# One contiguous run a partition for weights and output gates, and raw weight loads issued from ScalarE in an mLSTM + feed-forward kernel

## The chip, the cores and the metric

One core of one Trainium2 chip. The metric is the device time of the program in microseconds (us), the median over several executions. In the profile, PE is TensorE's matmuls and PEld its weight loads, DVE is VectorE, ACT ScalarE, POOL GpSimd, SP SyncE, which only issues transfers here. A name with a q behind it (SPq, ACTq) is that engine's instruction queue. Three engines issue transfers: SP, ScalarE and GpSimd.

## The reference, cut to what matters

```python
# mLSTM: batch 4, heads 8, 768 steps, head size 40
m_new = max(f + m, i);  f_stab = exp(f + m - m_new);  i_stab = exp(i - m_new)
C = f_stab * C + i_stab * outer(v, k);   n = f_stab * n + i_stab * k
y = sigmoid(o_gate) * (C q) / max(|n q|, 1)
# then on the 3072 x 320 result:
h = x @ w_in            # 320 x 2048
g = softplus(h)
out = g @ w_out         # 2048 x 320, float32 result
```

`w_in` and `w_out` arrive as float64; everything else is float32.

## The kernel before, in words

The 3072 tokens are cut into 24 steps of 128 (one batch and one chunk each; `ORDER` is their order), and three steps make a tile of 384 tokens. For each of the 8 tiles the feed-forward part runs over 16 blocks of 128 hidden columns: 8 matmuls of the block (L974, `hp`), softplus twice on ScalarE (L848, L849, `gh` and the full value), the remainder `gl` on VectorE (L852), and, two blocks later, 9 output matmuls (L942, `po`). A value is split into a high and a low part so that the fast matmul format keeps float32 accuracy.

The order of all work is written out by hand: TensorE's products of the blocks are counted (`tick(n)`), and every other piece of work is a generator that is resumed when the count reaches its place. `in_order` then fixes the order of the instructions on each engine as they were traced. So each engine, and SP's queue too, works strictly in this order: an instruction that waits holds what is behind it on its engine.

The mLSTM steps supply tile after tile. The first six (tiles 0 and 1) are plain steps, the others wide ones. For each step SP issues the decays `fb` (L421), two buffers of 128 partitions from a DRAM copy of the gates, which VectorE scans into the decay matrices `pw` (L430), further the queries and keys `qst`, `kst` (L369 and L370 in plain steps; in wide ones four copies of the high parts, L376, and two of the low parts, L390, from SBUF to SBUF) and the values `vt` (L405). The scores `sp` (L504) are multiplied into `pw` (L506). The wide steps' `iq` (L557), `y` (L560, L573) and `yq` (L568) give the step's output. `X` is the finished input of the feed-forward part: L619 (ScalarE) and L621 in plain steps, L605 and L607 in wide ones. `eg` holds the output gates of a tile, loaded from `oT` (L339) and put through a sigmoid (L345).

The weights are 16 tensors, 8 slices of `w_in` and 8 of `w_out`, each 128 partitions of 640 float64 values, loaded in the order of `tensors` into the raw buffers `wr` (three of them, `WB`, which the parts `lo` of tiles 3, 5 and 7 use later too). A slice of `w_in` takes three transfers (L221 once, L224 twice), a slice of `w_out` one (L227). A conversion (`single`, then `weights` or `weights_out`) makes float32 of the two 32-bit words of each value: ScalarE scales the high word into `mag` (L198) and the low word into `sg` (L201), VectorE puts in the sign from the high word (L203) and the shifted magnitude (L205). Then ScalarE casts the high part (L236, L240 or L251) and GpSimd forms the low part (L243, L245 or L253). The conversions run beside the blocks from 18 to about 129 us.

The first three loads are issued by `first_tile`, and its last line issues the fourth. After that a generator `fetch` stands beside each conversion and issues the next load, from SP, 8 counts behind the conversion's fourth piece of work, so behind L205, by which time the raw buffer has been read by ScalarE and VectorE.

A few transfers are issued by ScalarE already: `halves` (L1001, L1009) and most results `out` (L1022).

Of the kernel before, what the change touches and what calls it, by code (L numbers as in the profile page):

```python
# [8 lines left out]
F32 = mybir.dt.float32  # L9
F32R = mybir.dt.float32r  # L10
U32 = mybir.dt.uint32
AF = mybir.ActivationFunctionType
ALU = mybir.AluOpType
PSUM = bass.MemoryType.PSUM

B, H, S, D = 4, 8, 768, 40
L = 128
NG = 3
T = NG * L
NT = B * S // T  # L20
NC = S // L
HG = H // 2
DM = H * D
DFF = 2048
NF = DFF // 128
# [14 lines left out]
def mlstm_moe_kernel(  # L40
# [3 lines left out]
    vko: bass.AP,  # L44
    gates: bass.AP,
    oT: bass.AP,
    w_in: bass.AP,
    w_out: bass.AP,
    out: bass.AP,
):  # L50
    nc = tc.nc
    words = []
    if w_in.dtype != F32:
        words = [2]
        w_in = w_in.bitcast(U32).rearrange("r (f w) -> r f w", w=2)
        w_out = w_out.bitcast(U32).rearrange("r (e w) -> r e w", w=2)
    wdt = w_in.dtype

    cpool = ctx.enter_context(tc.tile_pool(name="cpool", bufs=1))
    p1 = ctx.enter_context(tc.tile_pool(name="p1", bufs=1))  # L60
# [129 lines left out]
    def single(src, n):  # L190

        if not words:
            return src
        lo_w, hi_w = src[:, :, :, 0], src[:, :, :, 1]
        shape = list(hi_w.shape)
        mag = stage.tile(shape, F32, tag="mag", bufs=MB, name=f"mag{n}")

        nc.scalar.activation(mag, hi_w.bitcast(F32), AF.Copy, scale=2.0**-112)  # L198
        yield
        sg = stage.tile(shape, U32, tag="sg", bufs=3, name=f"sg{n}")  # L200
        nc.scalar.activation(sg, lo_w, AF.Copy, scale=2.0**-29, bias=-0.4375)  # L201
        yield
        nc.vector.scalar_tensor_tensor(sg, hi_w, 0x80000000, sg, op0=ALU.bitwise_and, op1=ALU.bitwise_or)  # L203
        yield
        nc.vector.scalar_tensor_tensor(sg, mag.bitcast(U32), 3, sg, op0=ALU.logical_shift_left, op1=ALU.bitwise_or)  # L205
        yield
        return sg.bitcast(F32)

    def rows(a):
        return a.rearrange("(c p) f w -> p c f w" if words else "(c p) f -> p c f", p=128)  # L210

    WB, MB = 3, 2
    raw = {}

    def load_weights(u, i):
        if (u, i) in raw:
            return
        if i == 0:
            cs = slice(u * 256, (u + 1) * 256)
            r = stage.tile([128, 5, 128] + words, wdt, tag="wr", bufs=WB, name=f"wr{u}")  # L220
            nc.sync.dma_start(r[:, 0:4].rearrange("p (c j) f w -> p c (j f) w", c=2), rows(w_in[0:256, cs]))  # L221
            for j in range(2):
                f = 2 * u + j
                nc.sync.dma_start(r[j * 64 : (j + 1) * 64, 4], w_in[256:320, f * 128 : (f + 1) * 128])  # L224
        else:
            r = stage.tile([128, 2, DM] + words, wdt, tag="wr", bufs=WB, name=f"wo{u}")
            nc.sync.dma_start(r, rows(w_out[u * 256 : (u + 1) * 256]))  # L227
        raw[u, i] = r

    def weights(u):  # L230

        cs = slice(u * 256, (u + 1) * 256)
        w = yield from single(raw[u, 0], f"i{u}")
        w2 = w[:, 0:4].rearrange("p (c j) f -> p c (j f)", c=2)
        los = []
        nc.scalar.copy(wih[:, 0:2, cs], w2)  # L236
        for i in range(2):
            c1 = slice((2 * u + i) * 128, (2 * u + i + 1) * 128)
            hi, lo = slice(i * 64, (i + 1) * 64), slice((1 - i) * 64, (2 - i) * 64)
            nc.scalar.copy(wih[hi, 2, c1], w[hi, 4])  # L240
            los.append((wih[lo, 2, c1], w[hi, 4], wih[hi, 2, c1]))
        yield
        nc.gpsimd.tensor_tensor(wil[:, :, cs], w2, wih[:, 0:2, cs], op=ALU.subtract)  # L243
        for d, x, y in los:
            nc.gpsimd.tensor_tensor(d, x, y, op=ALU.subtract)  # L245
        yield

    def weights_out(u):
        w = yield from single(raw[u, 1], f"o{u}")
        js = slice(2 * u, 2 * u + 2)  # L250
        nc.scalar.copy(woh[:, js, :], w)  # L251
        yield
        nc.gpsimd.tensor_tensor(wol[:, js, :], w, woh[:, js, :], op=ALU.subtract)  # L253
        yield

    Cst = {}
# [78 lines left out]
    def wide_gates(t):  # L335

        yield 0
        eg[t] = p2.tile([128, NG, 3, L], F32, tag="eg", name=f"eg{t}")
        nc.sync.dma_start(  # L339
            eg[t].rearrange("p g c t -> p (g c) t"),  # L340
            oT[t * NG : (t + 1) * NG].rearrange("g (c p) t -> p (g c) t", p=128),
        )
        yield GL
        nc.scalar.preload_act_table_set("sigmoid_and_others")
        nc.scalar.activation(eg[t], eg[t], AF.Sigmoid)  # L345
        nc.scalar.preload_act_table_set("softplus")
        yield GL
# [3 lines left out]
    eg = {}  # L351
# [287 lines left out]
    def first_tile():  # L639
        zs = z0, z1, z2 = [Step(s) for s in range(NG)]  # L640
        run = lambda g: [None for _ in g]

        def part(g):
            for r in g:
                if not r:
                    return

        keep_warm(7)
        p0, lg = first_gates(), later_gates()
        next(p0)  # L650
        next(lg)
        load(z0)
        load(z1)
        next(p0)
        next(lg)
        nc.sync.dma_start(fz_d[0], fg0[:NCHAIN])
        og = p2.tile([128, NH, DM], F32, tag="X", bufs=XB, name="og")

        def output_gates(i0, i1):
            for i in range(i0, i1):  # L660
                b, c = ORDER[i]
                nc.sync.dma_start(og[:, i], vko[b, c * L : (c + 1) * L, H * E + DM :])
            yield
            nc.scalar.activation(og[:, i0:i1], og[:, i0:i1], AF.Sigmoid)
            yield

        o0, o1 = output_gates(0, NG), output_gates(NG, NH)
        next(o0)
        load(z2)
        load_weights(0, 0)  # L670
        next(o1)
        load_weights(1, 0)
        load_weights(0, 1)
        for z in zs:
            z.sig = og[:, z.g].rearrange("p (h d) -> p h d", d=D)
        v0, v1, v2 = (values(z) for z in zs)
        s0, s1, s2 = ([scores(z, i) for i in range(2)] for z in zs)
        x0, x1, x2 = (split_x(z) for z in zs)

        def mms(g):  # L680
            while next(g, None) == 1:
                pass

        def seq(*gs):
            for g in gs:
                next(g, None)

        decays(z0)
        run(p0)
        mms(s0[0])  # L690
        mms(s0[1])
        decays(z1)
        mms(s1[0])
        mms(s1[1])
        load(steps[NG])
        decays(steps[NG])
        gate_values(z0)
        next(lg)
        next(lg)
        nc.scalar.preload_act_table_set("sigmoid_and_others")  # L700
        put_off(lg, GR[2])
        gate_values(z1)
        decay(z0)
        last_decays(z0)
        seq(*s0)
        next(v0)
        decay(z1)
        last_decays(z1)
        decays(z2)
        seq(o0, wparts)  # L710
        next(v0)
        seq(*s1)
        next(v1)
        mms(s2[0])
        mms(s2[1])
        gate_values(z2)
        decay(z2)
        last_decays(z2)
        next(v0)
        next(x0)  # L720
        next(v1)
        seq(o1)
        nc.scalar.preload_act_table_set("softplus")
        seq(*s2)
        next(v2)
        next(x0)
        next(v1)
        next(x1)
        keep_warm(8)
        seq(x0)  # L730
        next(wparts)
        next(x1)
        next(v2)
        seq(x1)
        next(wparts)
        next(v2)
        next(x2)
        keep_warm(4)
        next(wparts)
        seq(wparts)  # L740
        next(x2)
        seq(x2)
        for _ in wparts:
            pass
        for z in zs:
            state_values(z)
        for i in range(NG, NH):
            nc.sync.dma_start(sgp[i], og[:, i])
        fetch_next()
        return zs  # L750

    def plain_step(z):
# [105 lines left out]
    def convert(u, i):  # L858
        g = (weights_out if i else weights)(u)
        for w in (CO if i else CW):  # L860
            yield w
            next(g, None)

    def fetch(i):
        yield (CO if i else CW)[3] + 8
        fetch_next()

    def fetch_next():
        if len(raw) < NF:
            load_weights(*tensors[len(raw)])  # L870
# [17 lines left out]
    def start(g, base):  # L888
        nonlocal order
        order += 1  # L890
        resume(g, base, 0, order)
# [142 lines left out]
    with in_order():  # L1034
        for k, (u, i) in enumerate(tensors[AHEAD:]):
            if k < 2:
                at = (-8, -2)[k]
            else:
                at = (17 - 2 * 34, 26 - 34 + 10 * (u == 4))[i] + 34 * u if u < SPLIT // 2 else (160, 180)[i] + 38 * (u - SPLIT // 2)
            start(convert(u, i), at)  # L1040
            start(fetch(i), at)
        start(first_states(), 0)
        LEAD, TS = 174, 16 * 17
        EARLIER = 26
# [55 lines left out]
```

## Time and profile before

| | |
|---|---|
| median of 3 runs | 495.0 us (493.74 to 495.5) |
| the profiled execution | 498.18 us, its span 496.4 us |
| TensorE matmuls busy | 473.1 us, 95% of the span |
| VectorE, ScalarE, GpSimd busy | 325.1, 216.6, 222.7 us |
| transfers from SP's queue (q1) | 67.82 MB, 44738 packets |
| transfers from ScalarE's queue (q10) | 4.43 MB, 3888 packets |

Rows of a timeline read: start, duration, engine, line, operation, tile written <- tiles read, shape, count; in brackets the idle time of that engine before it and what ended it. Rows of waits read: engine and line that waited <- what ended the wait: us in total, how often, the longest. A row of stretches gives the stretch, its length, the busy time of each engine with its instructions, the granted TensorE clock as a share of full speed (PEclk), the mean busy share of the 16 DMA engines, and what they moved. Rows of a tile give the line, engine, operation and count, then shortest/median/longest in ns, and the first and last start in us. Releasers are inferred: where an instruction waits for several things, the one named is the one that came last by the profile.

### The profile page before, as it was taken

To read this page: it belongs to the slowest core of one execution; us is meant where nothing else is said; L and a number is where in the kernel's file an instruction comes from. 1 tells how busy PE (TensorE), PEld (TensorE's weight loads), DVE (VectorE), ACT (ScalarE), POOL (GpSimd) and SP (SyncE) were. 2 spreads that over 40 slices of the span, in tenths; PEclk is the share of its full clock that TensorE was granted. 3 is DMA by queue.
4 is the path that set the end of the run, shared out by engine and by line. 5 is a ranking of instruction groups with operands and counts; after the bars stand their busy time and mean duration, and the time that the engine had idled before them with its cause. 6 is when DMAs were issued, how large, how long until landed. Compare 5 with 4: busy or idle time off the path is not lost.

```text
span 496.4 us, 9346 instructions
## 1 busy us (share of the span) xinstructions
PE 473.1 (95%) x3444; PEld 451.9 (91%) x3444; DVE 325.1 (65%) x517; ACT 216.6 (44%) x424; POOL 222.7 (45%) x303
## 2 busy tenths in 40 slices
PE   8997899895999999999999999999999999999997
PEld 8986798894998889999999999999999999999996
DVE  7877785689377676695587577578568567542211
ACT  1665544596224632536343534254343632333332
POOL 7375667387656324743355352643384244010000
PEclk9998898899799999999999999999999999999999
DMA  6946895769735877558856684569755572001001
GB/s 191 279 136 171 235 292 168 209 197 207 208 107 138 243 205 205 163 182 209 221 153 180 189 223 149 167 190 213 217 159 174 142 204 89 17 23 41 0 1 40
DMA packets 52991, 81.10 MB, mean 163 GB/s; under 512 B 7906, under 2 KB 31634, under 8 KB 52946
## 3 DMA queue, kind: packets, MB, share of 16 engines
q1 hardware_dynamic: 44738, 67.82, 48.7%
q0 software_dynamic: 4320, 8.26, 6.4%
q10 hardware_dynamic: 3888, 4.43, 2.7%
q8 instruction: 27, 0.44, 0.4%
q14 instruction: 18, 0.15, 0.1%
HBM read 52.38 MB, written 8.80 MB: 123 GB/s over the span
## 4 chain that ended last, share of the span: by engine, by line
PE 75%; DVE 10%; DMA 8%; ACT 3%; issue 2%; SPq 2%; ACTq 0%; DVEq 0%
PE hp L974 33%; PE po L942 31%; PE yq L568 3%; PE sp L504 3%; DVE pw L430 3%; DMA fb<-fz_d 3%; PE cp L481 2%; PE iq L557 2%; DMA lok<-in_qk 2%; DMA wr<-in_w_in 1%; DMA y<-fc_d 1%; DMA vt<-in_vko 1%; PE yp L538 1%; DVE sgo L203 1%; DVE gl L852 1%
## 5 line engine op out<-in xcount | busy, mean ns | idle before, releaser
L974 PE MATMUL hp<-X,wih 128*128 128x384 f32 x768 | 185.1, 345 | 3.0 <-ACT X L619 1.8
L974 PEld LDWEIGHTS hp<-X,wih 128*128 128x128 f32 x768 | 134.4, 191 | 6.1 <-ACT X L619 2.3
L848 ACT ACTIVATE gh<-hp 128x384 fp32r<-128x384 f32 x128 | 62.7, 490 | 175.0 <-PE hp L974 156.3
L852 DVE TENSOR_TENSOR gl<-hp,gh 128x384 fp32r<-128x384 f32 x128 | 70.2, 549 | 60.0 <-ACT hp L849 59.7
L942 PE MATMUL po<-woh,gl 128*128 128x320 f32 x384 | 84.2, 314 | 0.1
L942 PE MATMUL po<-woh,gh 128*128 128x320 f32 x384 | 84.1, 316 | 0.2
L942 PE MATMUL po<-wol,gh 128*128 128x320 f32 x384 | 83.1, 316 | 0.0
L430 DVE TENSOR_TENSOR_SCAN pw<-fb,ident 128x512 f32<-128x512 f32 x48 | 72.5, 1551 | 2.5 <-DMA fb<-fz_d 1.9
L974 PE MATMUL hp<-X,wil 128*128 128x384 f32 x256 | 70.0, 347 | 0.0
L942 PEld LDWEIGHTS po<-woh,gh 128*128 128x128 f32 x384 | 66.0, 190 | 1.6 <-ACT gh L848 0.4
L942 PEld LDWEIGHTS po<-woh,gl 128*128 128x128 f32 x384 | 63.5, 191 | 0.6 <-DVE gl L852 0.4
L942 PEld LDWEIGHTS po<-wol,gh 128*128 128x128 f32 x384 | 62.9, 191 | 1.0 <-issue 0.9
L849 ACT ACTIVATE hp<-hp 128x384 f32<-128x384 f32 x128 | 62.3, 487 | 0.0
L580 POOL DMA_DIRECT2D yd<-y x36 | 20.8, 579 | 89.5 <-DVE y L573 87.7
L974 PEld LDWEIGHTS hp<-X,wil 128*128 128x128 f32 x256 | 46.8, 191 | 1.1 <-issue 1.0
L560 DVE TENSOR_TENSOR y<-iq,y 41x512 f32<-41x512 f32 x36 | 24.5, 682 | 29.9 <-PE iq L557 28.7
L504 PEld LDWEIGHTS sp<-qst,kst 120*128 120x128 f32 (+1 forms) x240 | 33.8, 199 | 9.1 <-DVE sgo L203 5.1
L504 PE MATMUL sp<-qst,kst 120*128 120x128 f32 (+1 forms) x240 | 34.3, 278 | 8.0 <-DMA lok<-in_qk 4.8
L605 ACT CAST X<-eg 128x384 fp32r<-128x384 f32 x18 | 9.2, 513 | 59.2 <-DVE eg L603 59.2
L506 DVE TENSOR_TENSOR pw<-sp,pw 128x512 f32<-128x512 f32 x48 | 31.9, 680 | 4.1 <-PE sp L504 3.8
L486 DVE TENSOR_TENSOR cn<-cn,cp 40x328 f32<-40x328 f32 x16 | 7.8, 486 | 33.9 <-POOL cn L472 31.3
L457 POOL TENSOR_TENSOR vw<-vt,gw 128x328 f32<-128x328 f32 x19 | 16.7, 883 | 27.6 <-DVE gw L451 27.3
(131 smaller groups left out, 602.2 us busy)
## 6 DMA issues: line engine op xcount, KB each, us to landing
fb<-fz_d SPq DMA_DIRECT2D x42, 256.0 KB
vt<-in_vko SPq DMA_DIRECT2D x23, 324.0 KB
qst<-hiq SPq DMA_DIRECT2D x36, 160.0 KB
kst<-hik SPq DMA_DIRECT2D x36, 160.0 KB
wo<-in_w_out SPq DMA_DIRECT2D x8, 640.0 KB
wr<-in_w_in SPq DMA_DIRECT2D x8, 512.0 KB
eg<-in_oT SPq DMA_DIRECT2D x6, 576.0 KB
yd<-y POOLq DMA_DIRECT2D x36, 96.0 KB, 3.5
```

Of the source, the lines that this page charges most:

```text
L430: nc.vector.tensor_tensor_scan(pw.rearrange(flat), fb.rearrange(flat), ident4.rearrange(flat), 0.0, ALU.mult, ALU.add)
L457: nc.gpsimd.tensor_tensor(z.vw, v1, z.gw.broadcast_to([128, H, E]), op=ALU.mult)
L504: nc.tensor.matmul(sp[:, j, :], z.kst[:, h, :], z.qst[:, h, :], start=True, stop=True)
L506: nc.vector.tensor_tensor(z.pws[i], sp, z.pws[i], op=ALU.mult)
L560: nc.vector.tensor_tensor(y, iq, y, op=ALU.mult)
L568: nc.tensor.matmul(yq[e0:e1, p, :], z.via[:, h * E : h * E + e1 - e0], z.pws[h // HG][:, h % HG, :], start=True, stop=True)
L580: nc.gpsimd.dma_start(rows[i], z.y[i * PP : i * PP + EP])
L848: nc.scalar.activation(gh, hp, AF.Softplus)
L849: nc.scalar.activation(hp, hp, AF.Softplus)
L852: nc.vector.tensor_tensor(gl, hp, gh, op=ALU.subtract)
L942: nc.tensor.matmul(po[j], a[:, j * 128 : (j + 1) * 128], w[:, f, :], start=(first and left[j] == 2), stop=(last and left[j] == 0),)
L974: nc.tensor.matmul(hp, a, r, start=(i == 0), stop=(i == len(seq) - 1))
```

## The change

The weights lie in DRAM as one array `wts`, tensor by tensor, each with one contiguous run of 5,120 bytes a partition; so a load is one transfer for both kinds. `oT` is laid out the same way, one run of 4,608 bytes a partition for a tile. The loads from the fourth on are issued by ScalarE (`nc.scalar`) inside `single`, directly behind L201, the last read of the raw buffer by ScalarE. VectorE's sign operation takes the sign from `mag`, the scaled high word, so that VectorE no longer reads the raw buffer. The generators `fetch` and the fetch at the end of `first_tile` go. (The branches for `not words` are for float32 weights and do nothing here.)

```diff
         sg = stage.tile(shape, U32, tag="sg", bufs=3, name=f"sg{n}")
         nc.scalar.activation(sg, lo_w, AF.Copy, scale=2.0**-29, bias=-0.4375)
-        yield
-        nc.vector.scalar_tensor_tensor(sg, hi_w, 0x80000000, sg, op0=ALU.bitwise_and, op1=ALU.bitwise_or)
+        fetch_next()
+        yield
+        nc.vector.scalar_tensor_tensor(sg, mag.bitcast(U32), 0x80000000, sg, op0=ALU.bitwise_and, op1=ALU.bitwise_or)
         yield
...
-        if i == 0:
-            cs = slice(u * 256, (u + 1) * 256)
-            r = stage.tile([128, 5, 128] + words, wdt, tag="wr", bufs=WB, name=f"wr{u}")
-            nc.sync.dma_start(r[:, 0:4].rearrange("p (c j) f w -> p c (j f) w", c=2), rows(w_in[0:256, cs]))
-            for j in range(2):
-                f = 2 * u + j
-                nc.sync.dma_start(r[j * 64 : (j + 1) * 64, 4], w_in[256:320, f * 128 : (f + 1) * 128])
-        else:
-            r = stage.tile([128, 2, DM] + words, wdt, tag="wr", bufs=WB, name=f"wo{u}")
-            nc.sync.dma_start(r, rows(w_out[u * 256 : (u + 1) * 256]))
+        r = stage.tile([128, (2, 5)[i == 0], (DM, 128)[i == 0]] + words, wdt, tag="wr", bufs=WB, name=f"w{i}{u}")
+        (nc.scalar if len(raw) >= WB and words else nc.sync).dma_start(r.rearrange("p c f w -> p (c f w)" if words else "p c f -> p (c f)"), wts[2 * u + i])
         raw[u, i] = r
...
         nc.sync.dma_start(
-            eg[t].rearrange("p g c t -> p (g c) t"),
-            oT[t * NG : (t + 1) * NG].rearrange("g (c p) t -> p (g c) t", p=128),
+            eg[t].rearrange("p g c t -> p (g c t)"),
+            oT[t],
         )
...
             nc.sync.dma_start(sgp[i], og[:, i])
-        fetch_next()
         return zs
...
-    def fetch(i):
-        yield (CO if i else CW)[3] + 8
-        fetch_next()
-
     def fetch_next():
         if len(raw) < NF:
             load_weights(*tensors[len(raw)])
...
             start(convert(u, i), at)
-            start(fetch(i), at)
```

On the host the two weight arrays are transposed and stacked into `wts`, and `oT` is transposed.

More of the change, by code (lines that the diff above doesn't have):

```diff
@@ L46, in mlstm_moe_kernel @@
     oT: bass.AP,
-    w_in: bass.AP,
-    w_out: bass.AP,
+    wts: bass.AP,
     out: bass.AP,
@@ L52, in mlstm_moe_kernel @@
     words = []
-    if w_in.dtype != F32:
+    if wts.dtype != F32:
         words = [2]
-        w_in = w_in.bitcast(U32).rearrange("r (f w) -> r f w", w=2)
-        w_out = w_out.bitcast(U32).rearrange("r (e w) -> r e w", w=2)
-    wdt = w_in.dtype
+        wts = wts.bitcast(U32)
+    wdt = wts.dtype
     cpool = ctx.enter_context(tc.tile_pool(name="cpool", bufs=1))
@@ L207, in single @@
         return sg.bitcast(F32)
-    def rows(a):
-        return a.rearrange("(c p) f w -> p c f w" if words else "(c p) f -> p c f", p=128)
     WB, MB = 3, 2
@@ L245, in weights @@
             nc.gpsimd.tensor_tensor(d, x, y, op=ALU.subtract)
+        if not words:
+            fetch_next()
         yield
@@ L253, in weights_out @@
         nc.gpsimd.tensor_tensor(wol[:, js, :], w, woh[:, js, :], op=ALU.subtract)
+        if not words:
+            fetch_next()
         yield
@@ L1083 @@
         "gates": gates,
-        "oT": np.concatenate([oT, oT[:, DM - 64 :]], axis=1),
-        "w_in": inputs["moe_w_in"].reshape(H, D, DFF).transpose(1, 0, 2).reshape(DM, DFF),
-        "w_out": inputs["moe_w_out"],
-    }
+        "oT": np.concatenate([oT, oT[:, DM - 64 :]], axis=1).reshape(NT, NG, 3, 128, L).transpose(0, 3, 1, 2, 4).reshape(NT, 128, -1),
+    }
+    w = inputs["moe_w_in"].reshape(H, D, DFF).transpose(1, 0, 2).reshape(DM, NF // 2, 2, 128)
+    last = w[256:].transpose(2, 0, 1, 3).reshape(128, NF // 2, 1, 128)
+    w_in = np.concatenate([w[0:128], w[128:256], last], axis=2).transpose(1, 0, 2, 3)
+    w_out = inputs["moe_w_out"].reshape(NF // 2, 2, 128, DM).transpose(0, 2, 1, 3)
+    arrays["wts"] = np.stack([a.reshape(NF // 2, 128, -1) for a in (w_in, w_out)], axis=1).reshape(NF, 128, -1)
     arrays = {f"in_{n}": np.ascontiguousarray(a) for n, a in arrays.items()}
```

## The prediction

> **What bounds the kernel now.** I read the page first, then the table of stretches, then what TensorE waits for before and after 130 us, and last the timelines of the two stretches in which it waits for a transfer.
>
> ```profile
> span 496.4 us, 9346 instructions
> PE 473.1 (95%) x3444; PEld 451.9 (91%) x3444; DVE 325.1 (65%) x517; ACT 216.6 (44%) x424; POOL 222.7 (45%) x303
> ```
> ```profile
> core 0: us, PE busy (x) PEld busy (x) DVE busy (x) ACT busy (x) POOL busy (x), PEclk, DMA share, GB/s
> 30.00:40.00 10.00, 8.19 (x79) 7.09 (x77) 8.93 (x9) 6.25 (x12) 8.91 (x12) 1.00 0.14 42
> 60.00:70.00 10.00, 9.86 (x75) 9.06 (x75) 8.81 (x14) 5.25 (x10) 8.99 (x7) 0.88 1.02 261
> 100.00:110.00 10.00, 9.87 (x74) 9.09 (x74) 9.24 (x12) 9.92 (x15) 8.40 (x10) 1.00 0.64 203
> 120.00:130.00 10.00, 5.40 (x20) 5.43 (x21) 6.76 (x9) 3.85 (x8) 9.17 (x10) 0.69 0.87 212
> 200.00:300.00 100.00, 100.00 (x760) 96.20 (x759) 70.29 (x113) 44.13 (x86) 49.04 (x75) 1.00 0.70 192
> ```
> ```profile
> PE sp L504 <- DMA lok<-in_qk: 4.8, 1, 4.8
> PE pg L177 <- DVE d L168: 2.7, 1, 2.7
> PE sp L504 <- DVE pw L506: 2.2, 1, 2.2
> PE hp L974 <- ACT X L619: 1.8, 2, 1.5
> PE yq L568 <- DVE y L560: 1.5, 1, 1.5
> ```
>
> TensorE is the bound: busy for all of 200 to 300 us. It can only be made faster where it stands still, and that is where the weights are still being loaded and converted, up to about 130 us. The third fence (TensorE's waits from 20 to 130 us) sums to 13.0 us. After each long wait the granted clock is down too: 0.88 in 60 to 70 us, 0.69 in 120 to 130 us. What the change saves on VectorE, SP or the DMA engines counts only if it shortens one of those rows; what it adds on ScalarE counts only if it lengthens one.
>
> **Edits that I cost at nothing.**
>
> ```profile
> L224 SPq DMA_DIRECT2D wr<-in_w_in x16: 465/558/882, 11.5 to 96.4; - x16
> L203 DVE SCALAR_TENSOR_TENSOR sgo<-wo,sgo x8: 812/831/1352, 33.7 to 123.0; 128x640 uint32<-128x640 uint32 x8
> L205 DVE SCALAR_TENSOR_TENSOR sgo<-mago,sgo x8: 804/960/1605, 41.0 to 123.9; 128x640 uint32<-128x640 uint32 x8
> L339 SPq DMA_DIRECT2D eg<-in_oT x6: 478/486/1097, 91.4 to 374.6; - x6
> L345 ACT ACTIVATE eg<-eg x6: 1166/1167/1169, 107.0 to 387.1; 128x1152 f32<-128x1152 f32 x6
> ```
>
> The sign operation now reads the scaled word, as L205 does, in place of every second word. The minima are 812 and 804 ns, so the stride costs nothing to remove; with L205's median it would be 0.13 us dearer, 2 us over 16 and mostly beside TensorE's work. I take 0. The gates as one run: the first issue is at 91.4 us and the first reader at 107.0, so 15 us cover it; at most the issue time falls, and it could not lose more than those 15 us. The 16 second and third issues of the first weight matrix go (0.56 us each, 9 us of SP's time). For the three loads that stay on SP none of the waits above ends in a load, so 0. What these 9 us are worth later belongs to the stalls.
>
> **The stall at 58 us.**
>
> ```profile
> 39.38 0.35 SPq L166 DMA_DIRECT2D fz_d<-fg  x1
> 39.82 0.39 SPq L227 DMA_DIRECT2D wo<-in_w_out  x1
> 44.14 0.42 SPq L221 DMA_DIRECT2D wr<-in_w_in  x1
> 44.61 1.14 SPq L224 DMA_DIRECT2D wr<-in_w_in  x2
> 47.18 0.90 SPq L421 DMA_DIRECT2D fb<-fz_d  x2
> ```
> ```profile
> 31.68 0.79 ACT L201 ACTIVATE sgo<-wo 128x640 uint32<-128x640 uint32 x1
> ```
> ```profile
> 53.40 2.80 DVE L430 TENSOR_TENSOR_SCAN pw<-fb,ident 128x512 f32<-128x512 f32 x2 [1.87 <-DMA fb<-fz_d]
> ```
>
> Each conversion still issues the load three ahead of it; only the place in the conversion and the queue change. SP works in order. The decay broadcast fb is issued behind two weight loads, which themselves stand behind a store that waits for VectorE. The scan waits 1.87 us for fb, and the 2.2 us wait of the scores is the end of that chain (scan, product L506, scores). With the change the load of 44.14 is issued by ScalarE when its activation at 31.68 is done, at 32.5 us, and that of 39.82 one conversion before; both fall where the DMA share is 0.14. So fb is issued 0.42 + 1.14 = 1.6 us sooner and two loads of 655 KB (128 partitions of 5,120 B), 3.1 us each at the 212 GB/s of 120 to 130 us, no longer lie ahead of it. The scan can gain no more than its 1.87 us, the time for which VectorE stood idle before it. Bounds 0 and 1.9; I take 1.6. With a wait of 0.6 us left, the slow clock of 60 to 70 us (0.12 of 10 us, 1.2 us) should mostly go: 1.0.
>
> [...]
>
> **The stall at 120 us.**
>
> ```profile
> 103.32 0.37 SPq L227 DMA_DIRECT2D wo<-in_w_out  x1
> 103.74 0.94 SPq L421 DMA_DIRECT2D fb<-fz_d  x2
> 110.23 0.39 SPq L227 DMA_DIRECT2D wo<-in_w_out  x1
> 111.92 0.73 SPq L390 DMA_DIRECT2D qst<-loq  x1
> ```
> ```profile
> 98.18 3.38 DVE L430 TENSOR_TENSOR_SCAN pw<-fb,ident 128x512 f32<-128x512 f32 x2
> ```
> ```profile
> 124.60 1.08 PE L504 MATMUL sp<-qst,kst 120*128 120x128 f32 x4 [4.83 <-DMA lok<-in_qk]
> ```
>
> The view names lok, which this matmul does not read; it reads qst, whose last part was issued at 111.92, so I read the wait as that transfer, late in a long queue. SP stood until 103.3 for a raw buffer, with everything for this step behind it, though fb's buffers were free when the scans of 98.18 ended, at 101.6: SP starts 2.1 us sooner. The loads of 103.32 and 110.23 go out at 102.2 and 103.9 (rows below), into a stretch whose DMA share is 0.64, so up to 3.6 us of engine time are free to be filled. I take 3.0: qst lands near 121.6. TensorE, 1.1 us later there (next part), is ready at 120.9, so 0.7 of 4.8 us stays: gain 4.1, bounds 0 and 4.8. Of the slow clock (0.31 of 10 us, 3.1 us at most, part of it inside the wait) I take 2.0.
>
> **What ScalarE pays.**
>
> ```profile
> 92.88 0.77 ACT L201 ACTIVATE sgi<-wr 128x640 uint32<-128x640 uint32 x1
> 93.55 0.46 ACT L619 CAST X<-xp 128x384 fp32r<-128x384 f32 x1
> 101.36 0.80 ACT L201 ACTIVATE sgo<-wo 128x640 uint32<-128x640 uint32 x1
> 101.51 0.34 ACTq L1001 DMA_DIRECT2D halves<-ob0h  x1
> 103.04 0.81 ACT L201 ACTIVATE sgi<-wr 128x640 uint32<-128x640 uint32 x1
> ```
> ```profile
> 113.05 0.82 DVE L203 SCALAR_TENSOR_TENSOR sgo<-wo,sgo 128x640 uint32<-128x640 uint32 x1 [0.53 <-ACT sgo L201]
> 114.65 0.68 DVE L560 TENSOR_TENSOR y<-iq,y 41x512 f32<-41x512 f32 x1
> ```
>
> Today the next activation starts 0.1 us before the last one ends (93.55 against 93.65), and an issue of 0.34 us hides behind a running one. A load behind its own last read cannot hide: it waits for that read's end, then 0.34 us of issue, so about 0.55 us for each of 13 loads, 7.2 us in all. ScalarE is idle more than half of the time; it shows where a wait of TensorE ends on ScalarE. At 93.6 the copy X L619 stands right behind the issue, and the 1.5 us wait for it becomes 2.0: +0.5. From 100 to 110 us ScalarE is busy 9.92 of 10, with two issues: +1.1, handed on by L203, which waits for ScalarE, and L560 behind it to the yq wait. The issues elsewhere: +0.3, half of one. Deeper clock dips behind these: 0 to 2, I take 0.8. Together 2.7.
>
> Sum: −(1.6 + 1.0 + 4.1 + 2.0) + 2.7 = −6.0 us. The pg wait of 2.7 is VectorE's and stays. From 200 us on there is no idle time left that could take the gain back, and the work before it hangs on TensorE's own progress. The profiled execution took 498.2 us (span 496.4), 3.2 above the median of 495.0; off the median the forecast is 489.0, as profiled about 492.
>
> **Rivals.**
>
> *Half of it.* Only one of the two stalls goes, because qst is late on its own path or fb waits for the store. For: qst is issued 8 us behind fb even now. Left are 2.6 − 0.8 or 6.1 − 2.7: 491.5 to 493.5, say 492.5.
>
> *Nothing moves.* The engines are shared, so loads in another queue take the same time out of fb and qst; only SP's 1.6 us of issue in front of fb are saved, against 1.9 us of issues on ScalarE: 495. For: the DMA share of 1.02 and 0.87 near both stalls; against: the idle DMA of 30 to 40 us. [...]
>
> *Slower: ScalarE is held at the issue.*
>
> ```profile
> 175.23 0.82 ACTq L1009 DMA_DIRECT2D ob<-halves  x2
> 176.10 0.49 ACT L848 ACTIVATE gh<-hp 128x384 fp32r<-128x384 f32 x1 [2.96 <-DMA out<-ob]
> ```
>
> Here an issue on ScalarE waited for an older transfer to land, and the softplus behind it stood 2.96 us. TensorE had blocks in hand then. If the three issues at 93.7, 102.2 and 103.9 are each held 3 us, X and yq come 9 us later, on top of 1.9 for the issues and 2 for the clock; the wait at 120 us then covers 5, and 2.6 come from the first stall: 495 + 12.9 − 7.6 = 500. It decides from about 6 us of holds. Against: before 103.3 SP waits and issues little, so few older transfers are in flight when these three go out.
>
> **How the numbers follow.** Forecast 489.0: 0.50, with its own range 485 to 492.5. Half: 0.17. Nothing: 0.15. Slower: 0.18. About 0.3% (1.5 us) can be told from no change. The forecast and nearly all of half are faster: 0.67; most of nothing is the same: 0.13; the rest slower: 0.20. The range runs from 484 (the upper bounds 1.9 + 1.2 + 4.8 + 3.1 = 11.0 and no cost on ScalarE) to 496.5 (nothing moves, and 1.5 for the clock), and leaves out most of the slower case.
>
> **What would show it.** Weight loads on ScalarE's queue at about 32.5, 102 and 104 us; fb issued near 45.5; the scan without a wait, at about 51.5; the sp wait at 58 under 1 us and the one at 120 under 1.5; yq's wait near 2.6; the clock of 120 to 130 us near 1. I am wrong if the sp wait at 120 stays above 3 us, or if softplus rows on ScalarE wait for a DMA before 110 us.

## The result, and the profile after

| | before | after |
|---|---|---|
| median of 4 executions each, us | 494.37 (491.11 to 495.50) | 499.35 (497.86 to 500.93) |
| profiled execution, us | 498.18 | 500.93 |
| its span, us | 496.4 | 498.9 |
| its mean granted TensorE clock | 0.979 | 0.972 |

The ratio of the times is 1.0104, 95% interval 1.0054 to 1.0153: slower, by about 5 us on the medians, where 6 us less were forecast. The ratios here and below leave out executions more than 1.5% above the fastest of the same kernel; the medians hold all of them.

The page's head and the busiest engine of the kernel after, as those of before stand in the prediction:

```profile
span 498.9 us, 9291 instructions
...
PE 474.1 (95%) x3444; PEld 453.1 (91%) x3444; DVE 324.8 (65%) x517; ACT 217.3 (44%) x424; POOL 222.7 (45%) x303
```

The table of stretches after (us, then busy time of PE, PEld, DVE, ACT and POOL with instructions, granted clock, DMA share, GB/s):

```profile
60.00:70.00 10.00, 9.01 (x64) 8.49 (x63) 8.29 (x11) 4.34 (x8) 7.62 (x6) 0.76 0.98 289
70.00:80.00 10.00, 10.00 (x45) 10.00 (x45) 6.21 (x11) 5.20 (x9) 3.66 (x5) 0.56 0.21 69
...
100.00:110.00 10.00, 9.32 (x64) 8.74 (x63) 8.76 (x12) 5.81 (x12) 4.30 (x4) 1.00 0.44 124
...
120.00:130.00 10.00, 7.67 (x49) 6.97 (x49) 8.60 (x13) 7.81 (x16) 6.31 (x7) 0.67 0.45 112
```

And what TensorE waits for from 20 to 130 us:

```profile
PE iq L549 <- DVE cn L478: 4.6, 1, 4.6
PE hp L961 <- ACT X L611: 4.0, 2, 3.6
PE pg L175 <- DVE d L166: 2.2, 1, 2.2
PE sp L496 <- DVE pw L498: 1.4, 1, 1.4
```

The 4.8 us that sp waited for a transfer is gone, and the 2.2 us behind pw are 1.4. In their place stand 4.6 us at iq, a product that before waited 0.27 us, and 4.0 us for X where there were 1.8. ScalarE, busy for 9.92 of the 10 us from 100 to 110 before, is busy for 5.81: it stands there. Where, its timeline after shows:

```profile
105.37 0.38 ACTq L215 DMA_DIRECT2D w<-in_wts  x1
...
106.98 0.78 ACT L199 ACTIVATE sgi<-w 128x640 uint32<-128x640 uint32 x1
...
112.52 0.33 ACTq L215 DMA_DIRECT2D w<-in_wts  x1
112.96 0.57 ACT L297 ACTIVATE cs<-cn,lowk 120x336 fp32r<-120x336 f32 x1 [5.20 <-DMA qst<-hiq]
...
119.88 0.49 ACT L839 ACTIVATE gh<-hp 128x384 fp32r<-128x384 f32 x1
```

The first of these rows is the load before the last, the third the last one. The last load is ready to be issued when ScalarE's read of its buffer ends, at 107.76 us. It is issued 4.76 us later, and the state copy cs and all that follows on ScalarE stand behind it. The bracket names a transfer of qst; the chain of the same kernel (start, length, what) names another:

```profile
105.15 0.71 SPq L324
...
105.92 6.53 DMA y<-fc_d
112.45 0.02 issue
112.47 0.02 ACTq L215
...
112.52 0.33 ACTq L215
```

I go by the chain: the y transfer that SP issued at 105.92 lands at 112.45, and the load's issue starts on ScalarE at 112.47. In the chains of e1 and e9 an issue on ScalarE follows the landing of the same transfer as closely: landed at 111.54, issue at 111.56, and 107.01 and 107.03; the bracket of e1 names y itself. By what rule the issue is tied to this transfer no run shows. How the hold reaches TensorE, VectorE's timeline after shows:

```profile
120.79 0.56 DVE L843 TENSOR_TENSOR gl<-hp,gh 128x384 fp32r<-128x384 f32 x1 [3.06 <-ACT hp L840]
121.26 0.48 DVE L478 TENSOR_TENSOR cn<-cn,cp 40x328 f32<-40x328 f32 x1
```

Behind the held copy ScalarE has the output gates with two table loads (114.95 to 118.71) and the weight copies, so the softplus of 119.88 is late; VectorE stands at gl for it, the new state cn stands behind gl, and iq, which reads that state, behind cn.

### The profile page after: what moved, and what is told of

Same layout as the page of the kernel before. It is cut to its first block, busy times and chain, and to the rows that moved or that the text cites. A ratio compares the mean times of both kernels' runs of the same rounds, so it can differ in the third digit from the quotient of the medians.

```text
span 498.9 us, 9291 instructions
## 1 busy us (share of the span) xinstructions
PE 474.1 (95%) x3444; PEld 453.1 (91%) x3444; DVE 324.8 (65%) x517; ACT 217.3 (44%) x424; POOL 222.7 (45%) x303
## 4 chain that ended last, share of the span: by engine, by line
PE 80%; DVE 11%; ACT 4%; issue 2%; DMA 1%; POOL 0%; ACTq 0%; SPq 0%; DVEq 0%; POOLq 0%
PE hp L961 33%; PE po L929 30%; PE sp L496 4%; PE yq L560 3%; DVE pw L422 3%; PE cp L473 2%; PE yp L530 2%; PE iq L549 2%; DMA y<-fc_d 1%; PE fb L408 1%; DVE sgo L202 1%; PE ip L520 1%; DVE gl L843 1%; DVE sgi L202 1%; PE wm L622 1%
## 5 line engine op out<-in xcount | busy, mean ns | idle before, releaser
L422 DVE TENSOR_TENSOR_SCAN pw<-fb,ident 128x512 f32<-128x512 f32 x48 | 73.7, 1575 | 0.5 <-PE fb L408 0.5
```

Source lines behind the costliest of these rows:

```text
L422: nc.vector.tensor_tensor_scan(pw.rearrange(flat), fb.rearrange(flat), ident4.rearrange(flat), 0.0, ALU.mult, ALU.add)
```

## The experiments

Theory 1: the early places are good and the loss is the hold at the last load, ScalarE standing at an issue that waits for an older transfer. Theory 2: the early place itself, transfers crowding each other, or the drains lose the time; a drain is the short stop of ScalarE at an issue that must wait for the end of ScalarE's own read ahead of it (0.41 us of idle time at the load of 95.38 in the change). Theory 3: the granted clock, 0.76 and 0.56 from 60 to 80 us where it had been 0.88 and 1.00, loses it. Each of e1 to e12 is compared with the kernel before on the same chip. "Hold" is ScalarE's longest idle time at an issue between 95 and 122 us as the trace gives it, the issue itself included, "iq" TensorE's wait there, "clock" the mean over all executions of the run. The change has four executions, e4 eight, e6 six, every other run twelve.

| run | median us | ratio to before, 95% | hold | iq | clock |
|---|---|---|---|---|---|
| the change | 499.35 | 1.0104 (1.0054 to 1.0153) | 5.20 | 4.56 | 0.975 |
| e1, last load from SP, old place | 497.69 | 1.0047 (1.0013 to 1.0080) | 2.45 | 2.88 | 0.976 |
| e2, all loads from SP, old places | 494.86 | 0.9995 (0.9962 to 1.0028) | 0 | 0.25 | 0.978 |
| e3, ScalarE, old places | 496.21 | 1.0006 (0.9975 to 1.0037) | 1.28 | 1.53 | 0.976 |
| e4, eight products added | 499.67 | 1.0086 (1.0053 to 1.0120) | 5.35 | 4.56 | 0.980 |
| e5, last two early from GpSimd | 493.35 | 0.9935 (0.9903 to 0.9966) | 0 | none | 0.982 |
| e6, all early from SP | 490.04 | 0.9898 (0.9851 to 0.9945) | 0 | 0.25 | 0.989 |
| e7, five early, rest late | 498.99 | 1.0062 (1.0028 to 1.0095) | 1.22 | 1.50 | 0.977 |
| e8, eleven early, rest late | 497.76 | 1.0031 (1.0003 to 1.0059) | 4.29 | 4.55 | 0.977 |
| e9, all early from SP but the last two | 497.33 | 1.0044 (1.0012 to 1.0077) | 4.78 | 4.56 | 0.979 |
| e10, e6 again | 492.89 | 0.9961 (0.9925 to 0.9997) | 0 | 0.23 | 0.983 |
| e11, all early from GpSimd | 497.14 | 1.0039 (1.0005 to 1.0073) | 0 | none | 0.976 |
| e12, eleven on ScalarE, last two from SP | 494.80 | 0.9977 (0.9935 to 1.0018) | 0 | 0.29 | 0.981 |

The wait at iq follows the hold up to about 4.5 us and is 0.3 or nothing where there is no hold. (The profile of e5 is of an execution of 498.1 us, 4.8 above that run's median; only the absence of the wait is taken from it.)

**e1: the last load from SP at its old place.**

```diff
-        fetch_next()
+        if n != "i6":
+            fetch_next()
...
-        (nc.scalar if len(raw) >= WB and words else nc.sync)
+        (nc.scalar if WB <= len(raw) < NF - 1 and words else nc.sync)
...
+            if (u, i) == (6, 0):
+                start(fetch(i), at)
```

> The changed kernel, but the last of the 13 loads goes back to SP and to its old place in the order. Theory 1 (ScalarE is held at the issue of the last load, 107.8 to 112.5 us in the changed kernel, by an older transfer that has not landed): the iq wait of 4.6 us goes, cs and softplus behind it come about 5 us sooner, and the time falls by 3 to 6 us, to 494 to 496. Theory 2 (ScalarE pays for the drained issue of every load): 12 of 13 issues are left, so 498.5 to 499.5. Theory 3 (TensorE's clock falls at 64 us): unchanged, 499.

Measured: 497.69 us, between the two expectations. ScalarE's timeline of e1 tells why:

```profile
111.61 0.33 ACTq L993 DMA_DIRECT2D halves<-ob0h  x1
111.97 1.28 ACT L337 ACT_TABLE_LOAD   x1 [2.45 <-DMA y<-fc_d]
```

The third store of halves is held in the load's stead, until the same y transfer has landed at 111.54, by the chain of e1. About half of the loss went with about half of the hold.

**e2 and e3: the old places, from SP and from ScalarE.** Layout and sign stay as in the change; the generator `fetch` of before is back. e3 differs from e2 only in the queue.

```diff
-        fetch_next()        # in single, behind the last read
...
+        fetch_next()        # at the end of first_tile
...
+            start(fetch(i), at)
-        (nc.scalar if len(raw) >= WB and words else nc.sync)
+        nc.sync             # e2 only
```

> The new layout and the new sign operation alone: every load from SP at the place it had before. All three theories put the loss on the early issue from ScalarE, so this should be 0 to 3 us faster than before (491.5 to 494.5), from fewer transfers on SP. If layout or sign do harm themselves it stays near 499.

> The changed kernel, with every load still from ScalarE but at the old place, some 5 us behind its last read, so that ScalarE has nothing of its own to wait for. Theory 2: the drains are gone and the time falls by 2 to 4 us, to 495 to 497. Theory 1: the last load is issued near the landing of the older transfer, the hold shrinks below 1 us, 494 to 497; other issues may be held instead, and then softplus or X show a wait for a DMA. Theory 3: the scan at 51 us loses its gain, and with it the fall of the clock at 64 us: 495 to 497. The waits and the clock tell these apart.

Both take the time of before, within about 0.3%. So layout, sign and gates are worth nothing that shows here, as the prediction had it (the expectation for e2, 0 to 3 us faster, was met only at its lower end), and ScalarE's queue alone neither gains nor loses at places where no read has to be drained: 1.0006 against 0.9995. In e2 the stall at 120 us keeps most of its length under another name:

```profile
123.62 1.09 PE L495 MATMUL sp<-qst,kst 120*128 120x128 f32 x4 [3.33 <-DVE pw L421]
```

**e4: eight products before block 6**, to keep TensorE at work where the clock fell. Their result is overwritten. Each product is two instructions in the trace.

```diff
+            if k == 6:
+                for i in range(8):
+                    nc.tensor.matmul(hp[:, 0:128], ident, ident, start=True, stop=True)
```

> The changed kernel with 8 extra matmuls of the identity into block 6's own accumulator ahead of its first real product, where TensorE waits 1.0 us for the state of step 4 (extra work, no change of what is computed). Theory 3: the clock of 60 to 80 us, 0.76 and 0.56 in the changed kernel, stays near 1 and the time falls by 3 to 5 us, to 494.5 to 496.5. Theories 1 and 2: 0 to 0.5 us slower, 499.5.

The clock of 60 to 80 us is 1.00 in e4's profile, the hold and the iq wait are those of the change, and so is the time. The stretches, and the products, which themselves cost about 2 us:

```profile
60.00:70.00 10.00, 9.12 (x83) 8.58 (x82) 9.01 (x13) 5.06 (x10) 7.22 (x7) 1.00 0.99 268
70.00:80.00 10.00, 9.61 (x79) 8.74 (x77) 7.09 (x13) 6.58 (x12) 5.08 (x6) 1.00 0.42 148
```

```profile
63.48 1.95 PE L962 MATMUL hp<-ident 128*128 128x128 f32 x16
```

With the clock up the hold and the wait are still there, and the kernel is still slower than before. But the 2 us of the products hide what the clock may have given back, so e4 alone leaves some 2 us of the loss to theory 3; e12 below decides.

**e5: the last two loads early, from GpSimd.**

```diff
-        (nc.scalar if len(raw) >= WB and words else nc.sync)
+        (nc.gpsimd if len(raw) >= NF - 2 and words else nc.scalar if len(raw) >= WB and words else nc.sync)
```

> All of the change, but the last two weight loads are issued by GpSimd at the same early places; ScalarE keeps the other eleven. Theory 1 (the loss is the time that ScalarE sits at the issue of the last load, because an older transfer of decays lands at 112 us): ScalarE goes on behind its last raw read at about 107 us, the scaled state (cs) follows without the 5.2 us wait, iq waits under 2 us for cn, time 493 to 496, ratio 0.995 to 1.001. Rival 2 (the early places as such crowd the transfers at 105 to 112 us, whoever issues them): iq still comes at about 121 us and the time is 498 to 500. Price to look for: GpSimd has two more issues, 0.6 to 1 us each, ahead of vw and cs.

The same places, another engine, and the kernel is faster than before. Nothing of ScalarE stands behind the two issues now, and its trace shows no hold from 95 to 122 us. The iq that waited 4.56 us in the change comes without a wait:

```profile
114.48 0.41 PE L549 MATMUL iq<-qst,cs 120*41 120x128 f32 x4
```

The early place is not the loss.

**e6 and e10: every load early, from SP.**

```diff
-        (nc.scalar if len(raw) >= WB and words else nc.sync)
+        nc.sync
```

> All of the change, but every weight load is issued by SP at the early place. Theory 1 (a hold costs what stands behind it on the engine that issues): SP stands until ScalarE has read the buffer, so fb, y and the q and k of the next step, which follow on SP, go out later: the fb of step 4 behind 107 us where it went out at about 105; the stall at 120 us comes back as a wait for a DMA of 3 to 5 us; ScalarE is not held. Time 495 to 499. Rival 2 (only the place counts, not the engine): as the change, 499 to 500, with iq at about 121 us.

> The same kernel as the run with all loads early on SP, a second time. If its granted clock belongs to the kernel, most runs show a mean clock of about 0.99 and 489 to 491 us again. If the high clock was chance of that place and hour, the runs spread over 0.972 to 0.993 as those of the other kernels do, and the mean is 491 to 495 us.

The fastest version, and faster than before in both runs, in e10 by an interval that nearly reaches 1. My expectation for e6 was wrong: SP does stand for ScalarE's reads (25 us in seven waits of a load for L199), but ScalarE, not held, ends them sooner. Both last loads are out by 102.03, ahead of fb:

```profile
100.02 2.01 SPq L215 DMA_DIRECT2D w<-in_wts  x2
102.13 0.86 SPq L413 DMA_DIRECT2D fb<-fz_d  x2
103.04 0.71 SPq L324 DMA_DIRECT2D y<-fc_d  x1
```

That is SP's timeline of e6; before, the same fb went out at 103.74, between the two loads. The two stalls in e6, on TensorE's timeline:

```profile
56.65 1.16 PE L496 MATMUL sp<-qst,kst 128*128 128x128 f32 x8 [1.46 <-DVE pw L498]
...
118.21 0.63 PE L496 MATMUL sp<-qst,kst 120*128 120x128 f32 x4 [0.61 <-DMA loq<-in_qk]
```

e10 shows that the clock of e6 was in part luck: its twelve executions spread over 489.9 to 500.2 us at mean clocks of 0.993 to 0.969.

**e7: five early, the rest at late places.**

```diff
-        fetch_next()
+        if n in ("i1", "o0", "i2", "o1", "i3"):
+            fetch_next()
...
+            if k >= 5:
+                start(fetch(i), at)
```

> All of the change, but only the first five of ScalarE's loads (up to about 49 us) stand behind its own read; the other eight go out from ScalarE at the places of before. If the gain of the early issue at 58 us (1.1 us) reaches the end, the time is 493.5 to 495 and the ratio 0.996 to 0.999; if the waits for ScalarE's X and for the products swallow it as in the run with old places, the ratio is 0.999 to 1.002 (494.5 to 496.5). ScalarE is held for about 1.3 us at a later load, as in that run.

Slower than expected, and not for the reason tested: the edit also dropped the load of the first conversion, so that every load went out one conversion later than in either kernel. ScalarE then waits for the data:

```profile
105.83 0.78 ACT L196 ACTIVATE mago<-w 128x640 f32<-128x640 f32 x1 [2.81 <-DMA w<-in_wts]
...
120.36 0.78 ACT L196 ACTIVATE mago<-w 128x640 f32<-128x640 f32 x1 [2.17 <-DMA w<-in_wts]
```

It says what a late load costs, and nothing about the first five.

**e8: eleven early, the last two late, from ScalarE.**

```diff
-        fetch_next()
+        if n not in ("o5", "i7", "o6", "o7"):
+            fetch_next()
...
+            if k >= 11:
+                start(fetch(i), at)
```

> All of the change, but the last two loads go out from ScalarE at the places of before, some 20 counts behind the read; eleven stand early. Theory 1: the hold shrinks with the distance to the transfer of decays: ScalarE stands at a store of halves or at the last load for 1 to 4 us instead of 5.2, iq waits 1 to 3.5 us for cn instead of 4.6, time 495.5 to 498, in proportion. Rival 2 (the eleven early issues, with 0.4 us of drain each, carry the loss): 498 to 500 with iq at about 120 us all the same.

The hold is 4.29 us, longer than I thought, again at a store of halves that waits for y, and this time ahead of the table load instead of ahead of cs (104.42, not held). iq waits the same 4.55 us. So it is not cs that must come early, but whatever ScalarE does next.

**e9: all early from SP, the last two from ScalarE.** The counterpart of e5 and e6: one part of the change alone, put onto the fastest version.

```diff
-        (nc.scalar if len(raw) >= WB and words else nc.sync)
+        (nc.scalar if NF - 2 <= len(raw) and words else nc.sync)
```

> The run with all loads early on SP, but its last two loads go back to ScalarE: one part of the change alone, on top of the fastest version. [...] Rival 2 (the loss of the change lies in the eleven other issues, with 0.4 us of drain each): within 1.5 us of the run with all on SP, 489 to 492, iq without a wait.

497.33 against 492.89 us in e10, on the same chip: 4.4 us more, where rival 2 allowed 1.5. The hold is back, between the same y transfer and the same load as in the change, on ScalarE's timeline and in the chain:

```profile
101.97 0.78 ACT L199 ACTIVATE sgi<-w 128x640 uint32<-128x640 uint32 x1
107.08 0.34 ACTq L215 DMA_DIRECT2D w<-in_wts  x1
107.52 0.57 ACT L297 ACTIVATE cs<-cn,lowk 120x336 fp32r<-120x336 f32 x1 [4.78 <-DMA qst<-hiq]
```

```profile
100.55 6.46 DMA y<-fc_d
107.01 0.02 issue
107.03 0.02 ACTq L215
```

**e11: all early from GpSimd.**

```diff
-        (nc.scalar if len(raw) >= WB and words else nc.sync)
+        (nc.gpsimd if len(raw) >= WB and words else nc.sync)
```

> All thirteen loads early, but issued by GpSimd: neither SP nor ScalarE stands behind them. Theory 1: no hold on ScalarE, iq without a wait over 2 us, 489 to 495 us. Against it: each issue takes 0.6 to 1 us of GpSimd, 8 to 13 us in all, ahead of vw, vi and the low halves, so waits of TensorE for GpSimd (vw) may come to 2 to 5 us and the time to 494 to 498. A result of 498 or over would speak for the early place itself as the loss.

No hold, no wait at iq, and yet not faster than before. TensorE waits for GpSimd's low halves instead (po behind wol, 1.20 us at 55.19), and the profiled execution has a clock of 0.57 from 70 to 80 us. How much is the one and how much the other isn't told apart.

**e12: eleven early on ScalarE, the last two early from SP.**

```diff
-        (nc.scalar if len(raw) >= WB and words else nc.sync)
+        (nc.scalar if WB <= len(raw) < NF - 2 and words else nc.sync)
```

> The counterpart of the run with two loads on ScalarE: eleven early loads stay on ScalarE as in the change, and the last two go out early from SP. Theory 1 (the loss of the change sits in the hold at the last load): no hold, iq without a wait, sp of step 7 with a wait of 0.5 to 2 us, ratio 0.991 to 0.999 and 491 to 495 us, within 2 us of the run with all on SP; what is over that run is the price of eleven issues with their drains of 0.4 us on ScalarE. Rival 2 (the drains carry the loss): 497 to 500, X awaited over 4 us and the raw reads late.

This is the change with two loads moved, and its profiled execution happens to have the clock of the change's from 60 to 80 us:

```profile
60.00:70.00 10.00, 9.01 (x64) 8.49 (x63) 8.34 (x12) 4.38 (x8) 7.68 (x6) 0.76 0.96 284
70.00:80.00 10.00, 10.00 (x45) 10.00 (x45) 6.19 (x11) 5.15 (x9) 3.64 (x5) 0.56 0.23 70
```

Up to 105 us the two run within 0.1 us of each other (the first block behind X starts at 96.35 and 96.28). Then ScalarE and TensorE of e12:

```profile
106.28 0.80 ACT L199 ACTIVATE sgi<-w 128x640 uint32<-128x640 uint32 x1
106.97 0.58 ACT L297 ACTIVATE cs<-cn,lowk 120x336 fp32r<-120x336 f32 x1
```

```profile
118.72 1.08 PE L560 MATMUL yq<-pw,vi 128*64 128x128 f32 x16 [1.54 <-DVE y L552]
```

cs stands at 106.97 in place of 112.96, and yq comes at 118.72 in place of 124.68: 5.96 us. Of these 4.8 are the hold and 1.2 the two issues themselves: in the change L199 starts 0.70 us later (106.98 against 106.28), behind the drained issue of 105.37, and the rest is the last load's own issue ahead of cs. The spans are 492.8 and 498.9 us, 6.1 apart: all of it reaches the end. e9 and e6 are a second such pair: cs at 107.52 and 101.58, yq at 119.25 and 113.32, spans 493.1 and 487.9, 5.2 apart.

So theory 1 has the larger part, shown three ways: the hold goes when another engine issues the last loads (e5, e12), comes back when they alone are given to ScalarE (e9), and is handed on at its full size where the executions are otherwise alike. The drains of theory 2 have a smaller part, 1.2 of the 6.0 us at the last two loads; eleven early loads with their drains are no slower than before (e12). Theory 3 does not make the loss: e12 has the same low clock from 60 to 80 us, and not the loss.

## Why the prediction was wrong, point by point

**The stall at 58 us: right in its mechanism, smaller in size.** The rows after:

```profile
32.77 0.33 ACTq L215 DMA_DIRECT2D w<-in_wts  x1
```
```profile
45.13 0.90 SPq L413 DMA_DIRECT2D fb<-fz_d  x2
```
```profile
51.17 3.90 DVE L422 TENSOR_TENSOR_SCAN pw<-fb,ident 128x512 f32<-128x512 f32 x2
```
```profile
56.91 1.16 PE L496 MATMUL sp<-qst,kst 128*128 128x128 f32 x8 [1.42 <-DVE pw L498]
```

The load is on ScalarE's queue at 32.77 (32.5 foretold), fb goes out at 45.13 (45.5), and the scan starts at 51.17 with no wait (51.5). The matmul behind it starts at 56.91 instead of 58.04: 1.1 us, where I took 1.6. What is late next is VectorE's own scan and product, the 1.42 us that stay.

**The clock behind it: not to be had for the asking.** I priced 1.0 us for the clock of 60 to 70 us. It is 0.76 there after and 1.00 in e6, behind the same waits (1.42 and 0.99 us in the one, 1.46 and 0.99 in the other). One and the same program had 1.00 there in the profile of e6 and 0.83 in that of e10, so a clock read in one profile is no term of a sum.

**The stall at 120 us: right in its sum, and to the tenth partly by luck.** The outputs yq of two steps that follow each other, before and after the stall, in the change:

```profile
124.68 1.95 PE L560 MATMUL yq<-pw,vi 128*64 128x128 f32 x16 [0.53 <-DVE y L552]
...
142.99 1.09 PE L560 MATMUL yq<-pw,vi 128*64 128x128 f32 x16
```

And before:

```profile
115.47 1.08 PE L568 MATMUL yq<-pw,vi 128*64 128x128 f32 x16 [1.53 <-DVE y L560]
...
139.90 1.09 PE L568 MATMUL yq<-pw,vi 128*64 128x128 f32 x16
```

From the one to the other the change takes 18.3 us where before took 24.4: 6.1 us less, and 6.1 (4.1 of wait and 2.0 of clock) were forecast. In e6 it is 6.1 too (113.32 to 131.62), in e12 5.9 (118.72 to 137.22), but in e10, the same program as e6, 4.8 (114.99 to 134.58). Where sp of step 7 still waits there (e6, e12, e10) it is for 0.6, 1.7 and 1.9 us; 0.7 were foretold. So the wait fell by 3.0 to 4.2 us for the 4.1 of the forecast. In the change itself sp does not wait at all, because TensorE comes there 6 us later.

**What ScalarE pays: the step that failed.** The drains were priced rightly at X: it is waited for 3.11 us in e2 and e10, where ScalarE issues nothing there, and 3.62 in the change and e12: 0.51 for my 0.5. The rest of X's growth from 1.5 us is not the issue's; where it comes from stays open. In the change, and then in e10:

```profile
96.28 1.65 PE L961 MATMUL hp<-X,wih 128*128 128x384 f32 x4 [3.62 <-ACT X L611]
```
```profile
92.72 1.21 PE L961 MATMUL hp<-X,wih 128*128 128x384 f32 x4 [3.11 <-ACT X L611]
```

The 1.1 us for the two issues from 100 to 110 us came too, as the 1.2 by which cs is late beside the hold, though it does not stand in yq's own wait as I had it. But the sum of 2.7 held nothing for an issue that has to wait. I had that as the slower rival, with the right mechanism and a row of this kernel that shows it (a softplus 2.96 us behind an issue), gave it 0.18, and set it aside with one sentence: "before 103.3 SP waits and issues little, so few older transfers are in flight when these three go out". That sentence was read off the timeline of before, for the moment when the first of the three goes out. Two of the three were indeed free (95.38 and 105.37, right behind their reads). The third goes out at 107, and by then SP has just sent fb, y and q, the y transfer takes 6.53 us, and the load's issue starts only when it has landed (112.45, then 112.47). So the term that was put at nothing measures 4.8 us: one hold, not three of 3.

**The account.** At the first of those two outputs the change is 9.2 us behind before: 6.0 by the last two loads on ScalarE (e12 lacks them; 4.8 are the hold), and 3.2 that e12 shares. e6, with a clock of 1.00 from 60 to 80 us and no issue at X, is 2.2 ahead of before instead, near the 2.6 forecast for the first stall. Of the 5.4 us between e12 and e6, 0.5 are the issue at X; the other 4.9 came with the clock, as far as two profiles can tell. Then the stall at 120 gives 6.1 back, 3.1 remain at the second output, and 2.5 at the end of the span. So the last two loads ate the second gain whole, and the clock of that execution, as far as can be told, the first. The rival let the loss decide from about 6 us of holds; 4.8 us decided, with the 1.2 of the two issues beside them. The rival's 500 us was near the 499.35 measured by luck: it had three holds of 3 us, and its 2 us for the clock stood behind them and not at 60 to 80 us.

**What the forecast would have been worth without the hold.** e12 is the change less the hold and less the two issues that cost 1.2 us: ratio 0.9977, interval 0.9935 to 1.0018, so about 1 us of the forecast 6, at most 3. e6 and e10, which have no drains at all, come to 0.9898 and 0.9961, 5.1 and 2.0 us. Part of that is the clock: over 106 executions of the kernel before, the mean granted clock runs from 0.967 to 0.989, the time from 491.2 to 502.0 us, and they go together (correlation -0.83, 4.2 us for each 0.01). At equal clock the 18 executions of e6 and e10 are 0.6 us faster than before (interval -0.1 to 1.3), e9 is 1.5 slower (0.9 to 2.1) and the change 1.8 slower (0.8 to 2.7). By the same line e2 and e3, with the old places, are 1.3 and 1.4 us faster than before, so at equal clock the early places are not shown to beat the old ones. But the clock is also lower behind the long wait at iq (0.67 from 120 to 130 us in the change, 1.00 in e12, which has no such wait), so this split tells less than the ratios.

**The signs that I named.** The fb at 45.5, the scan at 51.5 and the sp wait under 1.5 us at 120 came; the sp wait at 58 us was to be under 1 us and is 1.42, and the loads of 102 and 104 us went out at 105.37 and 112.52. "Softplus rows on ScalarE wait for a DMA before 110 us" was close: it was cs, and the wait began at 107.8. The yq wait of 2.6 us is 0.5, because the wait moved to iq ahead of it; the clock of 120 to 130 us is 0.67, not near 1.

## What to carry to other kernels

Before a transfer is moved to an engine that also computes, list the older transfers that will still be on their way when it is issued at its new place, and when each will land, and price an issue that waits for one of them: here 4.8 us, for a transfer that took 6.53. A free-looking queue in the profile of before says nothing about the transfers that the change brings nearer. SP's 25 us of waits at its loads in e6 cost nothing that shows, while ScalarE's 4.8 us at one load were handed on in full to what stood behind it; by the medians the same early places gained 2 to 5 us from SP, the clock's share among them, and cost 5 us from ScalarE. Where a kernel's own executions differ by 2% with the granted clock, a pair of profiles with the same clock in the same stretches shows the size of one cause better than two medians.

## What the runs showed of the hardware that was not expected

The granted clock fell to 0.56 with no long wait ahead of it: between 30 and 64 us TensorE's longest wait in the change is 2.22 us, and it ends at 40.7. TensorE's timeline of the change, and then of e6:

```profile
64.08 2.73 PE L520 MATMUL ip<-cn,qst 128*128 128x42 f32 x16 [0.99 <-DVE cn L478]
```
```profile
63.82 1.98 PE L520 MATMUL ip<-cn,qst 128*128 128x42 f32 x16 [0.99 <-DVE cn L478]
```

Behind the same wait of 0.99 us the sixteen matmuls take 2.73 us in the one and 1.98 in the other, and the clock of the change is 0.56 from 70 to 80 us still. The mean clocks of e6 and e10, one program, differ from run to run, from 0.969 to 0.993. What sets off a single fall stays open.

A transfer of decays issued at 105.92 us took 6.53 us to land, and 6.46 in e9, while loads and q, k and v were under way behind it; the hold lasts until it lands. Why this one takes so long was not tried.
